# Gated linear attention into a routed expert layer: a table in its own tile, another order of loads, and ScalarE's and VectorE's order in the first steps

## The chip, the cores and the metric

The kernel runs on one core of one Trainium2 chip. Such a core has five engines that each work through their own queue in order: TensorE (PE, matrix products), VectorE (DVE), ScalarE (ACT, functions such as exp and ln), GpSimd (POOL) and SyncE (SP, which here only issues loads and stores). They wait for each other through semaphores; an instruction that waits holds up all that stands behind it on its engine. 16 DMA engines move data between the device memory (HBM) and the on-chip memory (SBUF). TensorE writes into PSUM, a small memory[...]. The metric is the device time of one launch in microseconds (us).

## The reference

Two blocks follow one another. The first is attention with a decaying state: for each of 4 batches and 8 heads, 768 tokens of width 48,

```python
f = 1.0 / (1.0 + np.exp(-f_logit))
for t in range(S):
    state = f[:, :, t, :, None] * state + np.einsum('bhd,bhe->bhde', k[:, :, t], v[:, :, t])
    y[:, :, t] = np.einsum('bhd,bhde->bhe', q[:, :, t], state)
```

Its output, 3072 rows of 384, goes into a layer of 8 experts. Each row takes the expert with the largest logit of `x @ w_gate`, with the softmax weight of that expert, and yields `gate_w * (relu(x @ w1[e]) @ w2[e])`, w1 being 384 x 1024 and w2 1024 x 384. All is in float32.

## The kernel before

**Units.** The attention is cut into 12 units: a unit is one chunk of 128 tokens of two batches, all 8 heads. Its q, k and f are tiles of 128 partitions x 8 segments x 128 tokens (512 KB each), its v is 384 KB. Within a chunk the recurrence becomes matrix products. For unit u:

- `steps` (L486, its exp at L492 and its ln, `log`, at L500): ScalarE makes ln(1 + exp(-f)), the decay of each token; `part` is a half of the segments, and `ab` names both halves.
- `total` (L502, instruction at L507): VectorE's running sum of it, a scan.
- `growth` (L516): ScalarE's exp of the sum, the tile r. `by_r` (L523): k times r, in place. It runs on GpSimd but for unit 0. `decay` (L533): exp of minus the sum. `by_decay` (L545): q times that, on VectorE.
- `ends` (L530) and `last_decay` (L540): small copies on GpSimd.
- `score` (L553): 32 matrix products of q and k. `mask` (L563): VectorE copies the causal half out of PSUM, in four instructions. `within` (L581): scores times v, the part of the output from the own chunk, in two halves.
- `keys` (L567), `keep` (L577): k is transposed on TensorE, and copied to SBUF by ScalarE.
- `added` (L617, PE dp): the state that the chunk adds; `update` (L633): VectorE adds it to the old state, GpSimd multiplies by the last decay. `before` (L596): q times the old state.
- `settle` (L645): ScalarE copies the output out of PSUM. `rows` (L660): TensorE turns it into rows and makes the gate's logits with the same products (PE xp, L679); VectorE sums the logits (lg, L687). `lay` (L697): ScalarE copies the rows.
- `Route.choose`, `place`, `fill` (L222 to L271): small VectorE instructions that pick the expert and the place of each row, for two units at a time. `send` scatters the rows by GpSimd.

**Steps.** The loop of L817 is a software pipeline: step n works on `score` to `added` of unit n, on the preparation of units n+1 to n+3, and on the output of units n-1 and n-2. The order of the source lines is the order of each engine's queue (`manual_schedule`, L711); nothing is reordered afterwards. Ahead of the loop stand the preparation of units 0 to 2 and `warm` (L721), matrix products whose result is not used.

**Buffers that set the order.** f has 2 tiles, k and v 3, q 4; r and the copied output one. The PSUM tiles of `keys`, `rows` and `added` take turns in two slots (`turns`, L468), so `added` of a step waits until `lay` has copied the first rows tile of that step. SP issues the loads in the order of the `load` calls (L473); a load into a tile that is still being read waits, and holds up those behind it.

**Constants.** `fpack` holds the float constants side by side: the unit matrix `ident` first, and among the others the table "rows" of 4 x 112 columns, which has a unit matrix for each half of the partitions with room for the gate's weights around it. `load_gate` (L176) writes these weights into the table, and so waits for the load of the table. `mpack` is the causal mask.

**`routed`.** L526 to L528 tie a k times r to an earlier VectorE instruction: it does not start before that has ended.

**After the attention** each expert's rows are read back, transposed and put through the two products by TensorE (L333, L349), with rows beyond the fixed regions in quarters of tiles (L1099, L1125). The change does not touch this.

## Time and profile before

| | |
|---|---|
| runs shown: median (lowest to highest of 3) | 394.76 us (393.43 to 395.92) |
| profiled execution: its time | 389.92 us |
| profiled execution: span from first to last instruction | 387.9 us |
| mean granted TensorE clock | 0.999 |
| TensorE busy | 375.7 us (97%) |
| VectorE busy | 169.3 us (44%) |
| ScalarE busy | 103.1 us (27%) |
| GpSimd busy | 116.0 us (30%) |
| moved by DMA | 95.04 MB |

The profile is of one execution. Its rows name an engine, a line of the kernel, an operation and the tiles it writes and reads, with the number of instructions and the time of one. In the timeline a row has its start and duration, and in brackets how long the engine had been idle and what ended that. SPq and POOLq are the DMA-issuing sides of these engines. A busy share is an average over the attention, which is over at about 125 us, and the experts; the stretch of the change is the first 45 us.

### The profile page before, as it was taken

What the parts mean: (1) busy time and instruction counts of PE and PEld (TensorE: products, weight loads), DVE (VectorE), ACT (ScalarE), POOL (GpSimd) and SP (SyncE); (2) the same over time, 40 slices, a digit from 0 to 9 for tenths busy, and PEclk for the clock granted to TensorE, in tenths of its full rate; (3) what the DMA queues carried; (4) which work ended last, traced back from release to release, by engine and by line L of the source; (5) the groups of instructions that cost most, each with busy time, mean ns of one, the idle gap of its engine ahead of it and who ended that gap; (6) DMA issues with size and microseconds to landing.
All of it is one profiled execution on the core that took longest, in us unless ns stands there. A gap on an engine that the chain in (4) does not pass through costs nothing.

```text
span 387.9 us, 7721 instructions
## 1 busy us (share of the span) xinstructions
PE 375.7 (97%) x3062; PEld 264.0 (68%) x3062; DVE 169.3 (44%) x365; ACT 103.1 (27%) x190; POOL 116.0 (30%) x118
## 2 busy tenths in 40 slices
PE   7899999999999999999999999999999999999994
PEld 7778899999989778685555555654466456555452
DVE  6899988889764632112121131115412113111260
ACT  6998878785433001010100110000010000001000
POOL 5378868887745410101102101100210210210112
PEclk9999999999999999999999999999999999999999
DMA  7999667778983459695659899899164449994151
GB/s 284 383 376 349 219 221 251 249 239 297 391 310 114 169 149 325 157 318 108 196 156 382 221 393 395 209 403 250 41 222 136 102 178 390 396 417 159 20 186 43
DMA packets 51515, 95.04 MB, mean 245 GB/s; under 512 B 20824, under 2 KB 40731, under 8 KB 49424
## 3 DMA queue, kind: packets, MB, share of 16 engines
q1 hardware_dynamic: 48016, 84.76, 64.4%
q0 software_dynamic: 3168, 9.64, 6.6%
q8 instruction: 25, 0.41, 0.5%
q14 instruction: 18, 0.15, 0.1%
q10 hardware_dynamic: 288, 0.08, 0.1%
HBM read 79.46 MB, written 15.21 MB: 244 GB/s over the span
## 4 chain that ended last, share of the span: by engine, by line
PE 88%; DMA 5%; DVE 2%; SPq 1%; issue 1%; ACT 1%; POOL 0%; POOLq 0%; DVEq 0%; ACTq 0%
PE hps L333 28%; PE yps L349 24%; PE yps L1125 7%; PE xp L679 6%; PE yt L587 5%; PE s L559 4%; PE s L333 3%; PE hps L1099 3%; PE yp L349 3%; PE yt L608 3%; DMA fpack<-c_fpack 2%; DMA f<-in_fu_dram 2%; PE dp L624 2%; PE kp L574 2%; DMA fpack<-in_moe_w_gate_dram 1%; SPq L482 1%
## 5 line engine op out<-in xcount | busy, mean ns | idle before, releaser
L333 PE MATMUL hps<-xT,w1t 128*128 128x352 f32 (+2 forms) x384 | 110.1, 447 | 0.0
L333 PEld LDWEIGHTS hps<-xT,w1t 128*128 128x128 f32 x384 | 72.7, 190 | 37.2 <-issue 1.9
L349 PE MATMUL yps<-w2t,hT 128*128 128x384 f32 x288 | 94.4, 487 | 0.0
L192 POOL DMA_INDIRECT out_dram<-ysb,dst x24 | 23.3, 972 | 224.4 <-DVE ysb L360 216.2
L349 PEld LDWEIGHTS yps<-w2t,hT 128*128 128x128 f32 x288 | 54.6, 190 | 38.6 <-issue 1.5
L343 ACT ACTIVATE hT<-hps 128x352 f32<-128x352 f32 (+2 forms) x28 | 13.7, 490 | 200.7 <-PE hps L333 190.6
L345 DVE TENSOR_SCALAR hT<-hps 128x352 f32<-128x352 f32 (+2 forms) x28 | 15.6, 558 | 93.0 <-PE hps L333 93.0
L360 DVE TENSOR_SCALAR ysb<-yps,tg 128x384 f32<-128x384 f32 x22 | 13.6, 618 | 74.4 <-PE yps L349 55.7
L192 POOL DMA_INDIRECT xs<-xr,posi x24 | 32.3, 1346 | 16.5 <-issue 4.8
L565 DVE COPY_PREDICATED at<-mpack,s 128x512 f32<-128x512 uint8 x48 | 31.1, 730 | 6.1 <-PE s L559 6.1
L525 POOL TENSOR_TENSOR k<-k,r 128x1024 f32<-128x1024 f32 (+1 forms) x12 | 26.6, 2217 | 19.2 <-ACT r L521 9.8
L507 DVE TENSOR_TENSOR_SCAN sum<-g,cap 128x1032 f32<-128x1032 f32 (+1 forms) x14 | 28.9, 2061 | 3.3 <-ACT g L500 3.2
L559 PE MATMUL s<-q,k 64*128 64x128 f32 x384 | 24.9, 279 | 2.4 <-POOL last L543 1.6
L1125 PE MATMUL yps<-qw,hqT 128*32 128x192 f32 (+1 forms) x192 | 26.8, 380 | 0.0
L679 PE MATMUL xp<-fpack,ys 128*128 128x104 f32 x192 | 25.1, 281 | 0.5 <-DMA fpack<-in_moe_w_gate_dram 0.3
L559 PEld LDWEIGHTS s<-q,k 64*128 64x128 f32 x384 | 22.5, 188 | 4.6 <-POOL last L543 1.8
L587 PE MATMUL yt<-at,v 128*48 128x128 f32 x384 | 25.1, 276 | 0.0
L679 PEld LDWEIGHTS xp<-fpack,ys 128*128 128x128 f32 x192 | 22.7, 191 | 2.4 <-issue 1.9
L587 PEld LDWEIGHTS yt<-at,v 128*48 128x48 f32 x384 | 20.0, 123 | 2.6 <-issue 1.3
L1125 PE MATMUL yps<-w2t,hT 128*32 128x384 f32 x192 | 21.4, 487 | 0.0
L1125 PEld LDWEIGHTS yps<-w2t,hT 128*32 128x32 f32 x192 | 7.6, 110 | 13.0 <-issue 12.5
L548 DVE TENSOR_TENSOR q<-q,g 128x1024 f32<-128x1024 f32 (+1 forms) x14 | 16.1, 1159 | 0.1
(114 smaller groups left out, 359.8 us busy)
## 6 DMA issues: line engine op xcount, KB each, us to landing
qw<-in_moe_w_dram SPq DMA_DIRECT2D x16, 1536.0 KB, 8.9
w1t<-in_moe_w_dram SPq DMA_DIRECT2D x8, 1536.0 KB, 7.5
w2t<-in_moe_w_dram SPq DMA_DIRECT2D x8, 1536.0 KB, 6.9
k<-in_ku_dram SPq DMA_DIRECT2D x12, 512.0 KB, 4.6
q<-in_qu_dram SPq DMA_DIRECT2D x12, 512.0 KB, 8.4
f<-in_fu_dram SPq DMA_DIRECT2D x11, 512.0 KB, 7.3
xs<-pad SPq DMA_DIRECT2D x8, 600.0 KB, 4.5
v<-in_vu_dram SPq DMA_DIRECT2D x12, 384.0 KB, 5.9
```

The costliest lines, as they stand in the source:

```text
L192: ins = nc.gpsimd.indirect_dma_start(out=dst, out_offset=bass.IndirectOffsetOnAxis(ap=idx, axis=0), in_=src, in_offset=None, bounds_check= ...
L333: nc.tensor.matmul(x["h"][:, f], lhsT=w[0][:, j, b * 128 : b * 128 + 128], rhs=x["xT"][:, j], start=j == 0, stop=j == KD - 1,)
L345: nc.vector.tensor_scalar(to, x["h"], 0.0, None, op0=OP.max)
L349: nc.tensor.matmul(yp, lhsT=x["hT"][:, f, t * C : t * C + C], rhs=w[1][:, f, :], start=f == 0, stop=f == NF - 1,)
L507: nc.vector.tensor_tensor_scan(x["sum"][:, part].rearrange("p s c -> p (s c)"), x["g"][:, part].rearrange("p s c -> p (s c)"), cap[:, part ...
L525: ins = on.tensor_tensor(k, k, units[u]["r"][:, part], op=OP.mult).ins
L548: nc.vector.tensor_tensor(q, q, x["dec"][:, part], op=OP.mult)
L559: done["score"] = nc.tensor.matmul(ps[h][:, p], lhsT=x["k"][r, s], rhs=x["q"][r, s], start=True, stop=True).ins
L565: nc.vector.copy_predicated(x["at"][:, a, h], _bc(causal, 1, HP), x["ps", a][h])
L587: nc.tensor.matmul(x["yt"][DP * (h ^ a) : DP * (h ^ a) + D, a, p], lhsT=x["v"][:, a, 2 * p + h], rhs=x["at"][:, a, h, p], start=p == 0, st ...
L679: done["rows"] = nc.tensor.matmul(xp[:, p], lhsT=x["ys"][:, a, p], rhs=wx[:, p, 0:XW] if a else wx[:, p, E:WX], start=True, stop=True,).ins
L1125: nc.tensor.matmul(yp[r], lhsT=h[:, f, at : at + T], rhs=w[:, f, cols], start=f == 0, stop=f == NF - 1, skip_group_check=True,)
```

## The change

The table "rows" leaves `fpack` and becomes a tile of its own, `wx`: GpSimd clears it at the start, and `lay_selection` copies the two unit matrices into it from `ident` once unit 0 is prepared. The gate's loads go into this tile. `ident` and `mpack` are loaded from SP's queue instead of ScalarE's. The order of loads becomes f0, k0, first half of f1, q0, second half of f1, ident, mpack, k1, q1 and so on; the gate is loaded ahead of f4, k3, q3, v2 and f5, the other constants after them.

In the preparation, q times decay of unit 0 comes after both halves of k times r. The masks of unit 0 are put between the halves of unit 1's preparation, whose second k times r waits for the first half's q times decay. `warm` has 8 products instead of 12.

In steps 1 to 3: k times r of unit 3 goes to VectorE, ahead of the last of step 2's four masks. exp and ln of units 4, 5 and 6 are issued apart: the ln of units 4 and 5 comes a step after the exp, that of unit 6 at the end of step 3, and in steps 2 and 3 they stand behind `lay`. `growth` of units 4 and 5 moves: that of unit 4 from step 2 into step 3, that of unit 5 to the end of step 3. `total(5)` and `choose` go behind `update(3)`, `settle(2)` from the start of step 4 to the end of step 3. Later steps are as before.

```diff
@@ -97,11 +97,6 @@
         "p": p[:, None],
         "sel": np.stack([p < DP, p >= DP], 1),
     }
-
-    sel = np.zeros((128, HP, WX))
-    for a in range(2):
-        sel[DP * a + np.arange(D), :, E + D * a + np.arange(D)] = 1.0
-    f["rows"] = sel.reshape(128, HP * WX)
 
     for n in (1, 2, 4):
         f[f"run{n}"] = row(np.tile(np.arange(n + 1) > 0, E))
@@ -161,13 +156,20 @@
     rend = cpool.tile([128, NU, SEG], F32, name="rend")
     gsum = cpool.tile([128, NU, 2], F32, name="gsum")
     pad = cpool.tile([128, ROW], F32, name="pad")
-    wx = const("rows").rearrange("p (h w) -> p h w", w=WX)
+    wx = cpool.tile([128, HP, WX], F32, name="wx")
     halves = [(a, slice(DP * a, DP * a + D)) for a in range(2)]
     fdram = nc.inline_tensor(fv, name="c_fpack").ap()
 
     def load_first_consts():
-        nc.scalar.dma_start(mpack, nc.inline_tensor(mv, name="c_mpack").ap())
-        nc.scalar.dma_start(ident, fdram[:, slice(*fat["ident"])])
+        nc.sync.dma_start(ident, fdram[:, slice(*fat["ident"])])
+        nc.sync.dma_start(mpack, nc.inline_tensor(mv, name="c_mpack").ap())
+
+    def lay_selection():
+
+        for a, r in halves:
+            nc.gpsimd.tensor_copy(
+                wx[r, :, E + D * a : E + D * a + D], _bc(ident[r, DP * a : DP * a + D], 1, HP)
+            )
 
     def load_consts():
         at = fat["ident"][1]
@@ -184,6 +186,7 @@
 
     nc.gpsimd.memset(pad, 0.0)
     nc.gpsimd.memset(pad[:, TOK : TOK + 1], float(FAR))
+    nc.gpsimd.memset(wx, 0.0)
 
     early_reads = []
     SYNC = mybir.DependencyInfo(mybir.DependencyClass.Sync, mybir.DependencyReason.DATA)
@@ -523,7 +526,7 @@
         def by_r(u, part=whole, on=nc.gpsimd):
             k = units[u]["k"][:, part]
             ins = on.tensor_tensor(k, k, units[u]["r"][:, part], op=OP.mult).ins
-            if routed:
+            if routed and on is nc.gpsimd:
 
                 tc.add_manual_dep(ins, routed.pop().name, SYNC, reason="the port of both")
 
@@ -545,7 +548,7 @@
         def by_decay(u, part=whole):
             x = units[u]
             q = x["q"][:, part]
-            nc.vector.tensor_tensor(q, q, x["dec"][:, part], op=OP.mult)
+            return nc.vector.tensor_tensor(q, q, x["dec"][:, part], op=OP.mult).ins
 
         def heads():
             return [(p, h, slice(DP * h, DP * h + DP)) for p in range(HP) for h in range(2)]
@@ -712,8 +715,10 @@
 
         nc.scalar.preload_act_table_set("natural_log_exp_and_others")
         load(0, "f", ab)
-        load(0, "kq")
-        load(1, "f")
+        load(0, "k")
+        load(1, "f", ab[:1])
+        load(0, "q")
+        load(1, "f", ab[1:])
         load_first_consts()
         load(1, "kq")
         for i in (1, 0):
@@ -733,16 +738,18 @@
             growth(0, part)
             by_r(0, part, nc.vector)
             decay(0, part)
+        for part in ab:
             by_decay(0, part)
         ends(0)
         last_decay(0)
+        lay_selection()
         for part in ab:
             steps(1, part)
         load(3, "f")
         load(2, "k")
         load(1, "v")
         load(2, "q")
-        load(3, "q")
+        load_gate()
 
         def early_banks():
 
@@ -788,31 +795,31 @@
         score(0, 0)
         score(0, 1)
         keys(0)
-        warm(12)
+        warm(8)
         for part in ab:
             total(1, part)
-        for a in range(2):
+        for a, part in enumerate(ab):
+            growth(1, part)
+            by_r(1, part)
+            decay(1, part)
             for h in range(2):
                 mask(0, a, h)
-        for part in ab:
-            growth(1, part)
-            by_r(1, part)
-        for part in ab:
-            decay(1, part)
-            by_decay(1, part)
+            scaled = by_decay(1, part)
+            if a == 0:
+                routed.append(scaled)
         ends(1)
         last_decay(1)
         steps(2)
+        load(4, "f")
+        load(3, "k")
+        load(3, "q")
+        load(2, "v")
         total(2)
         keep(0)
         steps(3, logs=False)
         growth(2)
+        load(5, "f")
         load_consts()
-        load(3, "k")
-        load(4, "f")
-        load(2, "v")
-        load(5, "f")
-        load_gate()
 
         for n in range(1, NU + 2):
             here, back, last = n, n - 1, n - 2
@@ -821,14 +828,14 @@
             rt = None
             if here < NU:
                 units[here]["old"] = states[here % 2]
-            if 2 <= last:
+            if 2 < last:
                 settle(last)
             if later and later[0] < NU - 1:
                 later[1].weigh()
             if here < NU:
                 for a in range(2):
                     score(here, a)
-            if ahead and n != 2:
+            if ahead and not 1 < n < 4:
                 by_r(n + 1)
                 ends(n + 1)
             if decayed:
@@ -850,28 +857,32 @@
             if state:
                 keys(here)
                 keep(here)
-            if n == 2:
+            if 1 < n < 4:
                 growth(n + 1)
-                by_r(n + 1)
+                if n == 3:
+                    by_r(n + 1)
                 ends(n + 1)
-            if 1 < n < 4:
                 decay(n + 1)
                 last_decay(n + 1)
             if here < NU:
                 for a in range(2):
                     for h in range(2):
+                        if n == 2 and a and h:
+                            by_r(n + 1, on=nc.vector)
                         mask(here, a, h)
             if n == 1:
                 log(3)
                 within(0, 0)
                 within(0, 1)
                 settle(0)
-            if n + 3 < NU:
+            if n == 1:
+                steps(4, logs=False)
+            elif n > 3 and n + 3 < NU:
                 steps(n + 3)
             if later and n >= NU - 1:
                 settled(*later)
                 later = None
-            if 2 < n < NU - 2:
+            if 3 < n < NU - 2:
                 total(n + 2)
             if n == NU - 2:
                 by_decay(n + 1)
@@ -881,6 +892,9 @@
             if 0 <= last:
                 rt = rows(last, later[1] if later else None)
                 lay(last)
+            if 1 < n < 4:
+                log(n + 2)
+                steps(n + 3, logs=False)
             if n == NU + 1:
                 scatter_some("rows")
             if later and n == NU - 2:
@@ -890,9 +904,9 @@
                 by_decay(n + 1)
             if n == 2:
                 total(n + 2)
-            if rt:
+            if rt and n != 3:
                 rt.choose()
-                if n < NU - 2:
+                if 3 < n < NU - 2:
                     routed.append(rt.latest)
                 if n >= NU - 1:
                     rt.weigh()
@@ -905,7 +919,7 @@
                     within(back, a)
             if n == 2:
                 settle(1)
-            if n + 2 < NU and n != 1:
+            if n + 2 < NU and n > 3:
                 growth(n + 2)
             if n == NU + 1:
                 widen(soon[0], weights[0], early_h, range(3, 7))
@@ -916,8 +930,16 @@
                 decayed = update(here)
             if n == 1:
                 total(3)
+            if n == 3:
+                total(5)
+                rt.choose()
+                routed.append(rt.latest)
             if back < NU:
                 before(back)
+            if n == 3:
+                settle(2)
+                log(6)
+                growth(5)
             if NU - 1 <= n <= NU:
                 scatter_some("before")
             if rt:
```

## The prediction

> **What bounds the kernel now.** I read the page first, for where TensorE (PE) stops being the only bound.
>
> ```profile
> span 387.9 us, 7721 instructions
> ...
> PE   7899999999999999999999999999999999999994
> ...
> DVE  6899988889764632112121131115412113111260
> ```
>
> Each digit is a tenth of one fortieth of the span, 9.7 us. PE is full from the third slice on; VectorE (DVE) is full in slices two to five, and near empty once the experts run. So the change, which touches the first 45 us, can only bring PE's full stretch forward. The chain that ended last, in order of time (start, duration, what), says who delays PE before that:
>
> ```profile
> 29.25 2.02 PE xp L679 x16
> 31.27 0.02 issue
> 31.29 0.04 DVE lg L687
> 31.33 0.07 issue
> 31.40 1.68 DVE q L548
> 33.08 1.16 DVE sum L507
> ...
> 38.26 1.97 DVE sum L507
> 40.22 0.78 issue
> 41.00 0.17 DVE lg L687
> 41.17 0.02 issue
> 41.19 0.49 ACT xr L709
> 41.68 0.04 issue
> 41.72 1.14 PE dp L624 x32
> ```
>
> From 41.72 the chain is PE work to the end, but for single microseconds. What is to be costed is therefore when `added(3)` (dp, L624) starts, and whether PE stays fed after it. Last the timeline (start, duration, engine, line; in brackets the idle time before):
>
> ```profile
> 9.81 0.64 ACT L492 ACTIVATE g<-f 128x512 f32<-128x512 f32 x1 [0.68 <-DMA f<-in_fu_dram]
> 11.22 2.51 DVE L507 TENSOR_TENSOR_SCAN sum<-g,cap 128x516 f32<-128x516 f32 x2 [0.73 <-ACT g L500]
> ...
> 36.53 2.38 POOL L525 TENSOR_TENSOR k<-k,r 128x1024 f32<-128x1024 f32 x1 [1.04 <-ACT r L521]
> 38.15 2.93 DVE L507 TENSOR_TENSOR_SCAN sum<-g,cap 128x1032 f32<-128x1032 f32 x1
> 47.50 2.29 DVE L507 TENSOR_TENSOR_SCAN sum<-g,cap 128x1032 f32<-128x1032 f32 x1
> ```
>
> VectorE works from 11.22 to 44.5 with only 1.4 us of gaps: it is the bound of this stretch. Its scan `total` (L507) takes 2.29 alone, and 2.93 where it starts while GpSimd's k times r (36.53 to 38.91) still has 0.76 to go; q times decay (L548) likewise 1.22 alone (at 50.46) and 1.68 at 31.40.
>
> **The change, part by part.** I walk VectorE's queue and shift it.
>
> *Loads.* The windows move 0.97 MB by 5.0 us and 2.88 MB by 10.0. f of unit 1 lands at 9.78; it and all ahead of it are 2.18 MB, reached at about 8.3, so a load lands some 1.5 us after its bytes' turn. In the new order f1's first half ends at 1.31 MB (turn 6.1, lands 7.6), q0 at 1.84 MB (8.9), f1's second half at 2.10 MB (9.6). ScalarE is busy until 9.12 with unit 0, so `steps(1)` starts at 9.12 instead of 9.81, and the first logarithm ends at 10.5 instead of 11.19. [...] The trace has the case: f0's first half was usable 3.2 us after its issue (exp at 4.02), while the whole f1 took 7.17. What counts is the first half's turn, so I take the trace: 0.7 us.
>
> q0's 0.18 MB more ahead of it costs 0.5; it was used at 8.59, so it lands by 9.05 at worst. q times decay of unit 0 now stands behind both k times r, at 9.3: covered by 0.3 us, beyond which each microsecond late is one on VectorE. ident and mpack move from ScalarE's queue into SP's at 2.1 MB and land near 9.8 instead of 4.9; first users are the `keys(0)` transposes at 11.7 and mask(0) at 13.0. Their two issues (0.43 each) hold k1 and q1 up in a queue that has 2 MB outstanding: nothing. The 448 columns less of the table are 0.23 MB, 0.6 us of transfer; nobody on the path waits for those bytes any more, so between 0 and 0.6, taken as 0. The gate's four loads (SP waited 2.7 us for the table ahead of them and issued until 24.5; landed 29.16) now wait only for a memset done by 5.5, and land near 20.5, ahead of `rows(0)`. They stand ahead of f4, k3, q3 and v2; beside the gate's packets throughput fell for 1 us from 344 to 229 GB/s, so I charge 0.6 us: f4 at 22.1, wanted at 24.1; k3 at 23.6, wanted at 28.6. The constants behind f5 land near 27.5, wanted by `choose` at 43 and by GpSimd's token copy, at 35.2 before. Nothing.
>
> *GpSimd.* memset of wx: 448 columns by pad's row (400 columns, 0.43) is 0.5, in an idle stretch from 4.7 to 8.0. Two copies of `lay_selection` are in no row: nearest is L531's small copy, 0.19 free and up to 2.2 when it is held up beside a scan. I take 0.3 each. GpSimd idled 3.27 us ahead of its k times r at 13.20; the cover is 1.5 us beyond ident's landing.
>
> *Steps 0 and 1.* total(1) then runs 10.5 to 13.0. mask(0) and q times decay by halves take 3.73 as before, to 16.75 (was 17.38). k times r of the second half now waits for the first q times decay (14.9) and ends at 16.4; behind it on GpSimd are only small copies until 20, and score(1) needs q at 16.7 anyway. warm(8) takes 8/12 of 2.84, so 1.9, ending at 14.7, before score(1) can start at 15.0. total(2) 16.8 to 19.1, mask(1) to 22.3, q times decay to 23.75, total(3) to 26.75, each about 0.95 earlier: 0.7 from f1 and 0.25 of gaps (17.38 to 17.66) closed.
>
> *Step 2.* k times r of unit 3 on VectorE: not in the trace. Below, twice the half at 0.62; above, L548 held up, 1.75. It is the same form as L548, so 1.22. It needs r, for which ScalarE goes through score(2) from 23.9, half of keys(2), keep(2) 1.05 and growth(3) 1.05, to 28.55; VectorE comes to it at 28.65 after three masks (0.65 each). So no wait, but a cover of only 0.1: a late r holds the fourth mask, both reductions and all behind. k times r to 29.9, fourth mask 30.5, first lg 30.7, lay's first copy 31.2. ScalarE's exp and log (2.2 us) no longer stand ahead of lay, and the gate no longer holds `rows(0)`: dp(2) starts at 31.2 (was 33.03). Then q times decay(3) to 32.1, not held up by GpSimd's k times r. log(4) now comes behind lay, 31.4 to 32.5, so total(4) waits 0.4 and runs 32.5 to 34.8 (was 33.00 to 35.30).
>
> *Step 3.* mask(3) to 37.8, lg to 38.65, with total(5) no longer ahead. PE took 8.69 from dp(2) to dp(3), 0.56 of it a stall for lay, which goes: dp(3) at 31.2 + 8.13 = 39.35 (was 41.72), **2.4 us** gained. But update(3), total(5), choose now stand in VectorE's queue behind dp(3), which ends at 40.5: 0.55 + 2.30 + 1.17, to 44.5, then mask(4) at 44.5 (was 45.01). What is late next is there: mask(4) 2.6, total(6) 2.3, lg 0.2, lay 0.5 set dp(4) at 50.05. PE alone would be there at 49.0. So 1.0 us is given back; dp(4) was at 51.15 to 51.3 and keeps some **1.3 us**. In step 5 PE's wide rows end after total(7), and dp(5) is not held: VectorE waits 0.6 us per step for scores in the later steps (row at 72.69), so it catches up.
>
> **The sum.** The profiled execution took 389.92, 387.9 of it the span: minus 1.3 to 1.4 gives 388.6. The runs shown have their median 4.84 above it, at 394.76; I carry the same difference over: **393.4**.
>
> **The rivals.**
> *No give-back.* If score and mask of step 4 overlap better, or total(5) starts before dp(3) has ended, the 2.4 us of dp(3) stay: 392.4. VectorE's own work caps this: 33.8 us from 11.22 to mask(4), less 1.9 idle, plus 1.22 for k times r, less 1.1 of hold-ups removed, is 32.0; from 10.5 that is 42.5, 2.5 earlier, and with lay's 0.85 of slack at dp(4) at most 3.3 us: 391.4. For it: the gaps I left in the queue sum to 1.9. Against: the order as written puts total(5) behind update(3).
>
> *VectorE pays (slower).* It is the bound, gets 1.22 more, and waits 0.4 for log(4) and up to 0.5 for dp(3). The walk has it 0.5 early at mask(4) only because 0.7 of f1 and 1.1 of hold-ups come off. If they don't (f1's half lands with the rest, GpSimd's copies still lie beside scans), mask(4) starts at 45.01 + 1.3 = 46.3 and dp(4) 5.6 later, at 51.9: 0.6 later than before, 395.4. It decides from mask(4) at 45.7 on (51.3 less 5.6); a late r adds one for one past 0.1. For it: VectorE's full digits, and a cover of 0.1. Against: f0's halves, and the 1.22 of L548 wherever GpSimd is quiet.
>
> *Nothing arrives at the end*, since a later stage waits for something else: 394.8. Against: PE has no gap from 42 to the experts, and the weights' loads follow PE's own releases.
>
> **How the numbers follow.** Forecast 393.4, 50%; no give-back 392.0 in the middle, 22%; VectorE pays 15%; nothing 13%. All of them lie within 1% of 394.76, which is about what a measurement of this kernel can tell from no change. More than 1% (3.9 us) needs more than the cap of 3.3, or the timed runs, which are slower than the profiled one, to gain more from early loads than the trace shows: 9%. Slower by 1% needs a head of a queue that is held for 5 us: 4%. Range 391.3 to 395.5: from the cap to most of the slower case.
>
> **What would show it.** Right: exp of unit 1 without idle at 9.1; scan of unit 1 at 10.5; no wait of xp for the gate; dp(2) near 31.2, dp(3) near 39.4, then a PE wait of about 1 us for lay at dp(4), near 50. Wrong: k times r of unit 3 waiting for r on VectorE, q0 holding VectorE at 9.3, PE waiting for lay at dp(5) too, or f4 landing after 24.

## The result, and the profile after

The changed kernel takes 392.83 us in the median of 22 runs (391.8 to 396.09), the kernel before 394.79 in 22 runs beside it (392.57 to 395.92): ratio 0.9965 [0.9949, 0.998], 1.96 us less. The forecast was 393.4, in a range of 391.3 to 395.5. The number was met. Much of its sum was not, and the experiments below are about that.

The page of the changed kernel; its profiled execution took 393.27 us:

```profile
span 391.5 us, 7712 instructions
...
DVE  6998998979663632112121131116413013111450
```

VectorE is still full in slices two to five, only in other slices of them. The span is 3.6 us longer than that of the profile before, in a kernel whose runs are faster. This is the first sign that the two profiles can't be subtracted: they come from chips of two kinds. On one kind the kernel before takes 389.7 us, on the other about 394 (the experiments below). By these times the profile before was taken on the first kind, the timed runs and the profile after on the second.

The chain that ended last, for the changed kernel (start, duration, what):

```profile
2.62 6.55 DMA q<-in_qu_dram
...
27.69 0.96 ACT r L524
...
31.03 0.55 ACT xr L707 x2
31.58 0.96 ACT g L503
...
32.63 0.06 DVE sum L510
...
41.60 2.30 DVE sum L510
...
44.98 2.51 DVE at L568 x4
47.49 1.78 DVE sum L510
49.27 0.40 issue
49.67 0.26 DVE lg L690 x2
```

Before, the chain became PE work at 41.72. Now VectorE's scans and masks carry it past 49.67, and it leaves them only in the next step. The new order brought step 2 forward, and VectorE then could not follow. The same in the timeline of the changed kernel (start, duration, engine, line; in brackets the idle time before):

```profile
8.64 0.61 ACT L495 ACTIVATE g<-f 128x512 f32<-128x512 f32 x1
9.19 1.29 DVE L551 TENSOR_TENSOR q<-q,g 128x512 f32<-128x512 f32 x2 [0.25 <-DMA q<-in_qu_dram]
10.40 2.60 DVE L510 TENSOR_TENSOR_SCAN sum<-g,cap 128x516 f32<-128x516 f32 x2
28.67 1.23 DVE L528 TENSOR_TENSOR k<-k,r 128x1024 f32<-128x1024 f32 x1
31.19 1.14 PE L627 MATMUL dp<-v,kn 128*64 128x48 f32 x32 [0.25 <-ACT xr L712]
32.63 2.31 DVE L510 TENSOR_TENSOR_SCAN sum<-g,cap 128x1032 f32<-128x1032 f32 x1 [0.78 <-ACT g L503]
35.45 0.66 PE L577 MATMUL kp<-fpack,k 128*128 128x128 f32 x4 [0.55 <-DVE state L644]
39.92 1.09 PE L627 MATMUL dp<-v,kn 128*64 128x48 f32 x32
46.72 1.14 PE L682 MATMUL xp<-wx,ys 128*128 128x104 f32 x8 [0.67 <-ACT kn L582]
50.40 1.14 PE L627 MATMUL dp<-v,kn 128*64 128x48 f32 x32 [0.19 <-ACT xr L712]
56.17 2.78 DVE L510 TENSOR_TENSOR_SCAN sum<-g,cap 128x1032 f32<-128x1032 f32 x1
59.60 1.14 PE L627 MATMUL dp<-v,kn 128*64 128x48 f32 x32
```

The `added` products of units 2 to 5 (L627; L624 before; dp(2) to dp(5) from here on) start at 31.19, 39.92, 50.40 and 59.60; before at 33.03, 41.72, 51.15 and 60.08. So 1.84 us is gained at the first, 1.80 at the second, 0.75 at the third, 0.48 at the fourth. PE's new waits are those for the PSUM slot that dp(2) had filled (35.45), for kn, the copy of k that ScalarE makes for unit 4 (46.72), and for lay (50.40). The second is no wait for VectorE: ScalarE works without a gap from 42.15 on, and has `settle(2)`, the logarithm of unit 6 and `growth(5)`, all put there by the change, ahead of this copy.

### The profile page after: what moved, and what is told of

Its sections match the earlier page's. It is cut to its first block, busy times and chain, and to the rows that moved or that the text cites. A ratio compares the mean times of both kernels' runs of the same rounds, so it can differ in the third digit from the quotient of the medians.

```text
span 391.5 us, 7712 instructions
## 1 busy us (share of the span) xinstructions
PE 377.9 (97%) x3054; PEld 264.7 (68%) x3054; DVE 171.0 (44%) x366; ACT 102.8 (26%) x190; POOL 113.7 (29%) x120
## 4 chain that ended last, share of the span: by engine, by line
PE 84%; DVE 8%; issue 2%; DMA 2%; ACT 1%; POOL 1%; SPq 0%; POOLq 0%; DVEq 0%; ACTq 0%
PE hps L336 28%; PE yps L352 24%; PE yps L1147 7%; PE xp L682 5%; PE yt L590 4%; PE s L562 4%; PE s L336 3%; DVE sum L510 3%; PE hps L1121 3%; PE yt L611 2%; PE yp L352 2%; DVE at L568 2%; DMA q<-in_qu_dram 2%; DVE q L551 1%; PE kp L577 1%
## 5 line engine op out<-in xcount | busy, mean ns | idle before, releaser
L528 POOL TENSOR_TENSOR k<-k,r 128x1024 f32<-128x1024 f32 (+1 forms) x11 | 24.1, 2190 | 14.1 <-ACT r L524 7.1
L682 PE MATMUL xp<-wx,ys 128*128 128x104 f32 x192 | 25.2, 281 | 0.9 <-ACT kn L582 0.7
L682 PEld LDWEIGHTS xp<-wx,ys 128*128 128x128 f32 x192 | 22.7, 191 | 2.8 <-issue 1.4
```

The source lines that it names most:

```text
L528: ins = on.tensor_tensor(k, k, units[u]["r"][:, part], op=OP.mult).ins
L682: done["rows"] = nc.tensor.matmul(xp[:, p], lhsT=x["ys"][:, a, p], rhs=wx[:, p, 0:XW] if a else wx[:, p, E:WX], start=True, stop=True,).ins
```

## The experiments

The theory after the result: the early gain is given back in steps 3 to 5, most of all on VectorE, and the timed difference has another source than that gain. The rivals: the timed difference is the gain at dp(4) and dp(5), plus something in the later kernel; or the difference belongs to the chip. The runs fell on chips of both kinds, so each is compared with the kernel before on its own chip, and starts only within one kind.

**Both kernels again (before2, after2, before3).** No edit: the kernel before twice more, the changed one once more.

> The kernel before, unchanged, looked at a second time, to see what repeats from one execution to the next. Theory (the prediction's): dp(2), dp(3) and dp(4) start at 33.0, 41.7 and 51.2 again, within 0.2, since every wait there comes from an order and from durations. Rival (a stall of TensorE that comes and goes in the later part decides the total): the starts up to 62 us repeat, but the time between the early expert tile and the end moves by 1 to 4 us.

> The changed kernel, unchanged, looked at a second time. Theory: dp(2), dp(3), dp(4), dp(5) at 31.2, 39.9, 50.4, 59.6 again, within 0.2. The wait of 1.3 us between the early tile's first and second product (near 127 us) and the lost 0.3 us in steps 5, 7 and 9 were in one profile: if they belong to the change they are there again, if they belong to the execution they are gone or elsewhere, and the span falls by some 2 to 3 us.

> The kernel before, unchanged, a third time, for the clock. The timed runs of before on the chip of the record fall into two groups, 392.6 to 394.0 with a granted clock of 0.995 or more and 394.2 to 395.7 mostly at 0.991 to 0.992. Theory [...]: where this execution is of the slow group, windows of 1 us show 0.50 in steps 2 to 3, score(3) takes 3.6 instead of 2.0, and dp(4) comes 1.7 us later than 51.1; where it is of the fast group, dp(2) to dp(4) are as before. Rival (the two groups come from the tail of the kernel): the clock is 1.00 up to 380 us in either case.

The first two ran on one chip of the first kind: before 389.72 (ratio to itself 1.0003 [0.9994, 1.0012]), changed 389.96 against 389.67, ratio 1.0006 [0.9997, 1.0015]. On this chip the change brings nothing. On a second chip of that kind before took 389.81 against 389.74, 0.9998 [0.999, 1.0005]. Timeline of the kernel before in its second profile:

```profile
33.00 1.14 PE L624 MATMUL dp<-v,kn 128*64 128x48 f32 x32 [1.13 <-ACT xr L709]
...
51.11 1.09 PE L624 MATMUL dp<-v,kn 128*64 128x48 f32 x32
...
60.04 1.09 PE L624 MATMUL dp<-v,kn 128*64 128x48 f32 x32
```

And of the changed kernel on the same chip:

```profile
31.48 1.14 PE L627 MATMUL dp<-v,kn 128*64 128x48 f32 x32 [0.24 <-ACT xr L712]
...
50.67 1.14 PE L627 MATMUL dp<-v,kn 128*64 128x48 f32 x32 [0.18 <-ACT xr L712]
...
56.48 2.75 DVE L510 TENSOR_TENSOR_SCAN sum<-g,cap 128x1032 f32<-128x1032 f32 x1
59.88 1.14 PE L627 MATMUL dp<-v,kn 128*64 128x48 f32 x32
```

The gain is 1.52 us at dp(2), 0.44 at dp(4), 0.16 at dp(5). These are pairs of single executions, which differ by as much: on the second chip of that kind the kernel before starts dp(2) at 33.57 and dp(5) at 60.60, some 0.56 later than above. In the changed kernel part of this spread has one source. q of unit 0 now stands behind half of f1, and VectorE waits for it, by 0.25 in the profile after, by 0.64 here, and by 0 to 0.86 in the edited kernels below; all that follows moves with it. At the first expert it is 0.11 (142.64 against 142.75), and at the end of PE still 0.11 (381.96 against 382.07). Yet the span is 0.7 longer. From the start of the last scatter on, 382.82 before and 382.72 after, the rest of the span takes 4.78 and 5.58. The queue of the instruction loads from 385 us on (number, MB, share of the DMA engines), before:

```profile
q14 instruction: 2, 0.02, 0.6%
```

and after:

```profile
q14 instruction: 3, 0.02, 0.7%
```

One more load of instructions falls into the end (five instead of four from the last scatter on). So 0.1 us of the span is gained on PE, and 0.8 lost behind it. Not all of this is in the time: between span and time lie 2.0 us in the runs of before and 1.8 in those of the changed kernel. The waits near 127 us and in steps 5, 7 and 9 that the profile after has are gone here, so they don't belong to the change.

**Three more GpSimd instructions, nothing else (pool3).** In the kernel before, three repeats of a small memset:

```diff
     nc.gpsimd.memset(pad, 0.0)
+    for _ in range(3):
+        nc.gpsimd.memset(pad[:, USED:ROW], 0.0)
```

> The kernel before with three small memsets more on GpSimd at its start, where it idles (columns of pad that are zero already). In all profiles so far the stretch from the last scatter's start to the end of the span is 4.8 to 5.0 us with four 8 KB instruction loads in it (before), and 5.4 to 5.8 with five (every kernel with the table's own tile, which has three GpSimd instructions more). Theory [...]: with three GpSimd instructions more the tail is 5.4 to 5.8 with five loads, and the time 0.4 to 0.6 above before. Rival (something else of the new tile makes the tail longer): 4.8 to 5.0, four loads, and the time of before.

Measured 393.25 against 393.67 on a chip of the second kind, 0.998 [0.9965, 0.9994]. The part of the span behind the last scatter (386.36 to 391.9) takes 5.54 with five instruction loads, as in the changed kernel, and not 4.8 to 5.1 with four. So three more GpSimd instructions are enough for a longer end. That the fifth load is what lengthens it is not shown: two edited kernels below, those with both edits at once and with the later scans moved, have four loads behind the last scatter and need 5.82 and 5.78 all the same. Nor do the runs show the price. A time 0.4 to 0.6 longer was expected, and the median fell by 0.4; part of before's runs on this chip are slow for another reason, taken up below, and the others have their median at 393.19, 0.06 below these.

**The halves of f of unit 1 undone (load_old).** On the changed kernel:

```diff
-        load(0, "k")
-        load(1, "f", ab[:1])
-        load(0, "q")
-        load(1, "f", ab[1:])
+        load(0, "kq")
+        load(1, "f")
```

> The changed kernel with the first loads in the old order (f0, k0, q0, f1 as one transfer). Theory (f1's first half is worth 0.7 us on VectorE): the exp of unit 1 starts at 9.7 to 9.8 instead of 8.6 to 9.1, its scan at 11.2, dp(2) near 31.9 and dp(4) near 51.0; the time 0.6 to 0.7 longer than the changed kernel's. Rival (it is absorbed by a gap further on): dp(2) stays at 31.2.

Measured 390.61 against 389.67 for the kernel before, 1.0023 [1.0015, 1.0031]. Timeline of this kernel:

```profile
32.26 1.14 PE L627 MATMUL dp<-v,kn 128*64 128x48 f32 x32 [0.24 <-ACT xr L712]
```

All dp start 0.78 to 0.79 us later than in the changed kernel on this chip, and the time is 0.65 longer. The split in two halves is worth its 0.7 us, and this gain comes through to the end undiminished. It would be larger if q of unit 0 came in time, for which VectorE does not wait here.

**k times r of unit 3 back on GpSimd (kr3_pool).** On the changed kernel:

```diff
-                if n == 3:
-                    by_r(n + 1)
+                by_r(n + 1)
                 ends(n + 1)
...
-                        if n == 2 and a and h:
-                            by_r(n + 1, on=nc.vector)
                         mask(here, a, h)
```

> The changed kernel with k times r of unit 3 back on GpSimd. Theory (the move trades 1.22 us of VectorE for two hold-ups and lands near nought): VectorE is free 1.2 us earlier for the fourth mask, q times decay of unit 3 is held up by GpSimd to 31.1 + 1.2, score(3) starts at 32.2 to 32.4 as with the move, total(4) 0 to 0.3 earlier; dp(4) at 50.1 to 50.4. Rival (the move is what brings the gain): dp(3) and dp(4) come 1 us later or more.

Measured 389.16 against 389.67, 0.9986 [0.9978, 0.9995]: 0.8 us faster than the changed kernel on the same chip, where the theory had nothing. Timeline of this kernel:

```profile
49.73 1.14 PE L627 MATMUL dp<-v,kn 128*64 128x48 f32 x32 [0.19 <-ACT xr L712]
...
58.93 1.14 PE L627 MATMUL dp<-v,kn 128*64 128x48 f32 x32
```

dp(4) is 0.94 us earlier than in the changed kernel, dp(5) 0.95. Of this 0.40 is there at dp(0) already (17.95 for 18.35), ahead of the edit, since VectorE waited only 0.18 for q of unit 0. That leaves 0.54. So the 1.23 us on VectorE cost 0.5 to 0.8 us. GpSimd's 2.4 us for the same product stand beside other work but for 0.45, for which PE waits at the scores of unit 3.

**The logarithm of unit 4 back ahead of lay (log4_early).** On the changed kernel:

```diff
             if n == 1:
-                steps(4, logs=False)
+                steps(4)
...
             if 1 < n < 4:
-                log(n + 2)
+                if n == 3:
+                    log(n + 2)
```

> The changed kernel with the ln of unit 4 right behind its exp in step 1, not behind lay in step 2. Theory (VectorE's gap ahead of total(4) is real loss on the bound): total(4) starts at 31.9 instead of 32.6, dp(3) near 39.3, dp(4) near 49.7, 0.7 earlier. Rival (ScalarE in step 1 is what it costs, keep(2) and growth(3) come later): k times r of unit 3 waits for r up to 0.6, and dp(4) is not earlier.

Measured 393.91 on a chip of the second kind, 0.9984 [0.9963, 1.0004]: unclear. Timeline of this kernel:

```profile
39.67 1.09 PE L627 MATMUL dp<-v,kn 128*64 128x48 f32 x32
...
50.23 1.14 PE L627 MATMUL dp<-v,kn 128*64 128x48 f32 x32 [0.19 <-ACT xr L712]
```

The first scores start at 10.52, and at 9.94 in the profile of the changed kernel, 0.58 later, as q of unit 0 came late by that much more. Taken from there, dp(2) (31.70) stands where it stood, dp(3) and dp(4) are 0.8 earlier. So the wait of `total(4)` for its logarithm, 0.78 in the timeline after, does cost what it says at dp(4); in the time it is not shown.

**Both at once (kr3_log4).** The last two edits together.

> The changed kernel with k times r of unit 3 back on GpSimd and the ln of unit 4 right behind its exp. Theory (both edits of the change put VectorE later, and each alone gave back 0.7 to 0.9 us at dp(4)): dp(2) near 30.7, dp(3) near 38.8, dp(4) 49.0 to 49.7, the time 1.0 to 1.6 us below the changed kernel's on the same chip. Rival (they give back the same gap once): dp(4) no earlier than 49.7, the time 0.8 below.

Measured 389.03 against 389.74, 0.9981 [0.9972, 0.9991], the lowest median of all. Timeline of this kernel:

```profile
50.12 1.14 PE L627 MATMUL dp<-v,kn 128*64 128x48 f32 x32 [0.20 <-ACT xr L712]
```

With both undone the kernel is 0.7 us below before, with k times r alone 0.5, on another chip, and the two intervals overlap. dp(0) starts at 18.36 here, as in the changed kernel's profile of this kind (18.35), and dp(4) 0.55 earlier than there: no more than the 0.54 of k times r alone. So the rival holds: the two edits of the change take away the same gap in VectorE's queue, once.

**The scan of unit 5 ahead of step 3's rows (tot5_old).** On the changed kernel, as the kernel before had it:

```diff
+            if n == 3:
+                log(5)
-            if 3 < n < NU - 2:
+            if 2 < n < NU - 2:
                 total(n + 2)
...
             if 1 < n < 4:
-                log(n + 2)
+                if n == 2:
+                    log(n + 2)
...
             if n == 3:
-                total(5)
                 rt.choose()
```

> The changed kernel with the ln and the scan of unit 5 back ahead of the logit sums of step 3. Theory (dp(3)'s gain is partly given back at dp(4) because the scan now stands behind update(3)): lg of step 3 waits for the scan, dp(3) starts near 40.9 instead of 39.9, but mask(4) starts near 43.8 instead of 44.9 and dp(4) near 50.0 instead of 50.4: the move of the scan is worth nothing or costs 0.4. Rival (the 2.4 us of dp(3) are the gain): dp(4) comes 0.5 to 1 us later than in the changed kernel.

Measured 398.18 against 394.04, 1.0102 [1.0065, 1.0138]: slower by more than any theory had it. Timeline of this kernel:

```profile
38.80 1.04 ACT L503 ACTIVATE g<-g 128x1024 f32<-128x1024 f32 x1
39.95 2.62 DVE L510 TENSOR_TENSOR_SCAN sum<-g,cap 128x1032 f32<-128x1032 f32 x1 [1.77 <-ACT g L503]
42.49 0.26 DVE L690 TENSOR_REDUCE lg<-xp 128x8 f32<-128x32 f32 x2
43.21 1.72 PE L627 MATMUL dp<-v,kn 128*64 128x48 f32 x32 [2.85 <-ACT xr L712]
46.75 3.75 PE L562 MATMUL s<-q,k 64*128 64x128 f32 x32
```

The logarithm comes only at 38.80, behind what ScalarE has to do in that step, so the scan waits 1.77 us at the head of VectorE's queue, with lg and lay behind it, and PE waits 2.85. Then something more happens: dp takes 1.72 instead of 1.14, the scores 3.75 instead of 2.06. The same kernel by stretches of time (length; busy time and instructions of PE, its weight loads, VectorE, ScalarE and GpSimd; the granted TensorE clock; DMA share; GB/s):

```profile
42.00:43.00 1.00, 0.00 (x0) 0.00 (x0) 1.00 (x4) 0.32 (x1) 0.68 (x2) 1.00 0.72 286
43.00:44.00 1.00, 0.79 (x20) 0.79 (x21) 0.88 (x1) 1.00 (x4) 0.00 (x0) 0.76 0.02 6
44.00:46.00 2.00, 2.00 (x42) 1.91 (x44) 0.96 (x4) 0.65 (x2) 0.00 (x0) 0.50 0.04 8
46.00:48.00 2.00, 2.00 (x28) 1.64 (x22) 0.56 (x4) 1.06 (x3) 0.00 (x0) 0.50 0.13 20
48.00:50.00 2.00, 2.00 (x22) 2.00 (x22) 1.14 (x2) 2.00 (x5) 0.00 (x1) 0.50 0.94 338
50.00:51.00 1.00, 1.00 (x11) 0.81 (x10) 0.67 (x2) 0.98 (x2) 1.00 (x1) 0.83 0.82 332
```

The clock was 0.50 from about 43.5 on, for some 6.8 us (estimated from the 0.76 and 0.83 at its ends). At half the clock this is a loss of about 3.4, by estimate. Two of the seven executions, with a mean clock of 0.998 and 0.999, took 396.5, so that without the fall this edit still costs some 3 us against the 393.5 of before's executions with a clock of 0.994 or more.

**The later scans behind lay (tot_late).** On the changed kernel:

```diff
-            if 3 < n < NU - 2:
-                total(n + 2)
             if n == NU - 2:
...
-            if n == 2:
+            if n == 2 or 3 < n < NU - 2:
                 total(n + 2)
```

> The changed kernel with the scan of steps 4 to 9 behind q times decay, as it is in step 2, instead of ahead of the logit sums. Theory (the scan of unit 6 ahead of the logit sums is what holds dp(4)): lg of step 4 at 48 to 49, dp(4) near 49.4 without a wait for lay, 1.0 earlier; in later steps VectorE, which has 0.3 to 0.6 us a step to spare, keeps up, and the whole is 0.5 to 1.0 us shorter than the changed kernel. Rival (VectorE's sum of work is the bound, so the wait only moves on): mask(5) and with it dp(5) come 1 us late instead, and the time is that of the changed kernel.

Measured 395.87, 1.0057 [1.0038, 1.0076]. Timeline of this kernel:

```profile
49.87 1.09 PE L627 MATMUL dp<-v,kn 128*64 128x48 f32 x32
...
59.20 1.13 PE L627 MATMUL dp<-v,kn 128*64 128x48 f32 x32
```

dp(4) and dp(5) start 0.53 and 0.40 earlier than in the profile after (0.17 of that is there at dp(2) already), and PE does not wait at dp(4). It still waits 0.67 for kn ahead of it, as in the changed kernel: with VectorE out of the way only 0.36 of the 1.05 comes back at dp(4), and what ScalarE's order costs there no run isolates. From dp(5) on the four intervals are 9.82, 9.35, 9.88 and 9.83 us, in the profile after 9.69, 8.93, 9.69 and 8.93. So the wait has only moved on, as the rival had it; it grows there, and the time is longer, not the same.

**The gate and the table's own tile, without the rest (gate_only).** On the kernel before (with the table taken out of the constants as in the change, not shown again):

```diff
+    nc.gpsimd.memset(wx, 0.0)
...
         last_decay(0)
+        lay_selection()
...
+        load_gate()
         load_consts()
         load(3, "k")
         load(4, "f")
         load(2, "v")
         load(5, "f")
-        load_gate()
```

> The kernel before with only the table's own tile: table out of the constants, gate's weights loaded ahead of the constants, all else in the old order. Theory: rows(0) no longer waits 0.3 us for the gate, but dp(2) is set by lay behind ScalarE's exp and ln, so dp(2) stays at 32.9 to 33.0, dp(4) at 51.1 to 51.3, and the time is the same within 0.2. Rival (the gate's late landing and SP held for 2.7 us are what the change removes): dp(2) and dp(4) 0.5 us earlier or more.

Measured 395.87 against 394.04, 1.004 [1.0018, 1.0063]: alone this part is slower, where both theories had no loss. Timeline of this kernel:

```profile
27.15 1.06 ACT L495 ACTIVATE g<-f 128x1024 f32<-128x1024 f32 x1 [2.45 <-DMA f<-in_fu_dram]
29.92 2.03 PE L682 MATMUL xp<-wx,ys 128*128 128x104 f32 x16 [1.27 <-ACT kn L582]
34.80 1.14 PE L627 MATMUL dp<-v,kn 128*64 128x48 f32 x32 [1.84 <-ACT xr L712]
35.87 3.69 PE L562 MATMUL s<-q,k 64*128 64x128 f32 x32
```

f of unit 4 stands behind the gate's loads and the constants here, and ScalarE waits 2.45 us for it. Its exponential starts at 27.15; in the kernel before at 25.38, in the changed kernel at 23.88 without a wait, since f4 is ahead of the constants there. PE then waits 1.27 and 1.84 us. The same kernel by stretches:

```profile
33.00:34.00 1.00, 0.00 (x0) 0.00 (x0) 1.00 (x1) 0.97 (x3) 1.00 (x2) 1.00 1.07 402
34.00:35.00 1.00, 0.20 (x6) 0.20 (x8) 1.00 (x2) 1.00 (x4) 1.00 (x2) 1.00 0.89 337
35.00:36.00 1.00, 1.00 (x34) 0.94 (x30) 1.00 (x1) 1.00 (x3) 1.00 (x1) 0.96 0.93 347
36.00:37.00 1.00, 1.00 (x10) 1.00 (x12) 1.00 (x2) 0.16 (x1) 1.00 (x2) 0.50 1.07 328
...
38.00:39.00 1.00, 1.00 (x12) 1.00 (x12) 1.00 (x2) 0.19 (x1) 0.73 (x1) 0.50 0.70 263
39.00:40.00 1.00, 1.00 (x12) 0.87 (x10) 0.73 (x2) 0.00 (x0) 1.00 (x1) 0.84 0.28 115
```

Again 0.50, from about 35.9 on for some 3.4 us (estimated from the 0.96 and 0.84 at its ends), and scores of 3.69 instead of 2.06. The six executions with a mean clock of 0.994 or more have their median at 394.9, those of before at 393.5: the late f4 costs without the fall too.

**A wait made longer in the kernel before (act_extra).** Three copies of 0.47 us on ScalarE ahead of lay in step 2:

```diff
+            if n == 2:
+                for _ in range(3):
+                    nc.scalar.copy(scr, cap.rearrange("p s c -> p (s c)")[:, 0:320])
             if 0 <= last:
                 rt = rows(last, later[1] if later else None)
```

> The kernel before with three idle ScalarE copies of 320 columns (some 1.1 us together) put ahead of lay in step 2, so that TensorE waits some 1.9 us for lay at dp(2) instead of 0.8. Theory [...]: in some or all executions the mean clock is 0.991 to 0.992, the profile shows 0.50 in steps 2 to 3 with score(3) at 3.6 us, and the time is 1.1 us above before without, and near 2.8 us above it with the fall[...]. Rival (the fall needs more than this, or another chip): clock as before, time 1.0 to 1.2 us above before in all executions.

Measured 395.03 against 393.67, 1.0026 [1.0001, 1.0051]. Timeline of this kernel:

```profile
32.55 1.42 ACT L884 COPY scr<-cap 128x320 f32<-128x320 f32 x3
...
34.41 1.14 PE L625 MATMUL dp<-v,kn 128*64 128x48 f32 x32 [2.06 <-ACT xr L710]
```

In this profile the clock did not fall. But of its 12 executions 8 have a mean clock of 0.989 to 0.993 and take 394.76 to 395.93; the other 4 have 0.995 to 0.997 and take 392.85 to 393.84. Of the kernel before on the same chip 10 of 31 lie below 0.994. So low means came more often with the longer wait, 8 of 12 against 10 of 31, and not in every execution; with so few executions this is at the edge of chance. The expected 1.1 us without the fall did not come: the median of the 4 is 393.31, that of before's 21 executions at 0.994 or more 393.19.

**What the profiles show of the clock.** In two of them it fell to 0.50 within the steps. In gate_only PE had waited 1.27 and 1.84 us ahead of it, in tot5_old 2.85. In the kernel with the three copies PE waited 2.06 us, and the clock stayed at 1.00:

```profile
32.00:34.00 2.00, 0.35 (x8) 0.09 (x2) 2.00 (x2) 1.94 (x5) 2.00 (x3) 1.00 1.04 383
34.00:36.00 2.00, 1.59 (x40) 1.54 (x42) 1.66 (x2) 2.00 (x6) 1.52 (x3) 1.00 0.94 306
36.00:38.00 2.00, 2.00 (x33) 1.88 (x30) 1.55 (x4) 0.72 (x1) 1.20 (x1) 1.00 1.02 404
```

So a wait of PE stood ahead of both falls, and one longer than gate_only's had no fall behind it. What lets the clock fall, and why some executions of a kernel have a low mean and others not, is not shown.

**What this says of the timed difference.** The runs of the record, sorted:

| | executions | up to 394 us | their median | above 394 us | their median |
|---|---|---|---|---|---|
| before | 22 | 9 | 393.09 | 13 | 395.23 |
| changed | 22 | 20 | 392.78 | 2 | 395.19 |

Between the lower groups there are 0.3 us. The other 1.65 of the 1.96 is that the median of before lies in its upper group, and that of the changed kernel in its lower one. Of before's runs here the clocks are not known, but on two chips of the second kind they are. On chip 3, 10 of its 31 executions have a mean clock below 0.994 (median 395.0) and 21 a higher one (393.19); on chip 7, 13 of 39 (394.70, the others 393.49). By estimate, one stretch like that of gate_only, 3.4 us at half the clock, costs 1.7 us, close to the 1.8 between the groups on chip 3, and lowers the mean clock by 0.5 x 3.4 / 388 = 0.0044, somewhat less than the 0.0055 between the groups' means. The mean is a rough sign: it takes in a fall behind the last product too (in after2 0.59 from 384 to 386 us and 0.50 from there on), where PE has nothing left to do, and after2 has a mean of 0.995. Of the changed kernel's 22 executions none lies below 0.994, and the two above 394 us have 0.994 and 0.998. On the two chips of the first kind no execution of either kernel lies below 0.994 (of load_old's 20 there one does, with 0.991 and 392.12 us), and there the change shows nothing.

Whether the new order removed falls of the clock is not shown. For it: it shortens PE's waits for lay in step 2 from 0.76 to 1.24 us (four profiles of before's order) to 0.25, and in step 3 from 0.55 to none. Against it: the kernel with three memsets, whose waits in these steps are those of before, has no mean below 0.994 among 20 executions; and log4_early, whose waits are as short as the changed kernel's, has 4 among 12. No profile caught the kernel before in a fall, so whether and where it has one is open. Nor is step 2 the only place where PE waits. All seven profiles of the second kind have PE waiting between 126 and 135 us, where the first expert products begin, by 0.8 to 1.75 us in all, and none of the first kind does. The row of the kernel with three memsets:

```profile
129.17 5.43 PE L351 MATMUL yp<-w2t,hT 128*128 128x384 f32 x16 [1.24 <-ACT hT L345]
```

Whether the clock falls there in any execution was not shown.

## Why the prediction was right or wrong

**The number was right by luck, and not by its sum.** The sum took 1.3 to 1.4 us off the profiled execution and carried the 4.84 us between it and the timed runs over as a constant. That is the step that failed. Some 3.4 of the 4.84 lie between the two kinds of chips (389.7 and the lower group's 393.09); most of the rest is that before's median lies in the upper group. On the first kind, that of the profile, the sum makes 388.6, and the changed kernel takes 389.96 there, 0.3 above before with an interval that takes in no difference. On the second kind 0.3 of the 1.3 us arrived between the lower groups. The rest of the 1.96 is that fewer runs lie in the upper group, for which the prediction had no term; that the clock is behind it is likely, and not shown for these runs.

**Loads: f1 right, q0 mis-sized.** The prediction had exp(1) at 9.1 and scan(1) at 10.5; they start at 8.64 and 10.40 (exp(0) too was earlier in that execution, 3.62 instead of 4.02). The split of f1, taken from f0's halves in the trace, was worth 0.65 to 0.8 us. For q of unit 0 it had a cover of 0.3 at 9.3. There was none: VectorE was ready at 8.94 and waited 0.25 in the profile after and 0.64 in after2, which is one of the signs of being wrong that it named. This load is on the chain that ended last.

**The gate at 0.6 us, too small.** In gate_only it stands ahead of f4, which ScalarE waits for in both kernels, and f4 comes 1.77 us later (27.15 for 25.38). The forecast came off unharmed: in the changed kernel f4 is ahead of the constants, and exp(4) starts at 23.88 without a wait.

**Step 2, right to the hundredth by luck in part.** dp(2) 31.19 for 31.2. k times r started at 28.67 for 28.65 and took 1.23 for 1.22. The cover of 0.1 was gone: the third mask ended at 28.60 and r at 28.64, so VectorE waited for r, if only for hundredths. On the chip of the profile before dp(2) starts at 31.48.

**k times r on VectorE, mis-sized.** It was walked through as one term among others and not priced alone. Alone it costs 0.54 us at dp(4) and 0.8 in the runs, and the kernel is faster without it.

**log(4) behind lay, 0.4 expected, 0.78 measured.** The logarithm ended at 32.53, as forecast (32.5); VectorE was free for it at 31.86 instead of 32.1. log4_early shows that the wait is paid in full at dp(3), as long as k times r stands on VectorE too.

**Step 3, 0.57 late.** dp(3) 39.92 for 39.35: the prediction's "8.13 of PE from dp(2) to dp(3)" had no wait in it, and there is one of 0.55. The second half of `keys(3)` waits for VectorE's update to read dp(2) and free its PSUM slot, and that update stands behind the late `total(4)`. The wait of lay did go, as predicted.

**The give-back, right in size, half right in kind.** The prediction had mask(4) at 44.5 and dp(4) at 50.05; they start at 44.90 and 50.40. PE's 10.48 from dp(3) to dp(4) is 1.05 more than before's 9.43, as the 1.0 of the forecast. But its kind is only half right: the forecast was one wait of about 1 us for lay, and PE waits 0.19 for lay and 0.67 for kn, which stands behind ScalarE's new order. ScalarE's queue at the end of step 3 had no term in the walk.

**"dp(5) is not held", wrong.** total(7) runs beside GpSimd's product and takes 2.78 (56.17), dp(5) is held by about 0.3 and keeps 0.48, on the other chip 0.16, and 0.11 at the experts. The prediction argued from VectorE's idle time in later steps, but dp(5) comes before these.

**The end, not thought of.** 5.4 to 5.8 us of span behind the last scatter instead of 4.8 to 5.1, less the 0.2 that is not in the time. That is some 0.45 (an estimate from these spans), more than PE keeps on the first kind of chip; pool3's runs show less, 0.06.

**Rivals.** "VectorE pays" named the mechanism that took the gain, with a price of 0.6 over before; on one chip of the first kind the changed kernel is 0.3 above before, in an interval that takes in no difference. "Nothing arrives at the end" is what that chip shows. "No give-back" falls.

## What to carry to other kernels

A stall removed ahead of the engine that is the bound is worth only what that engine can follow (1.84 us at dp(2) here, 0.48 of it left at dp(5)): walk its queue on until the gain is either kept for several steps or gone, and price each operation that is moved to it by itself. Ask of each load that is put ahead of another who waits for the other. Before the distance between a profile and timed runs is carried over, look whether both are of one chip and whether the runs have one group or two. Two versions within half a per cent are told apart only on the same chip (the kernel before took 389.7 us on the one kind and 393.7 to 394.8 on the other).

## What the runs showed of the hardware

- **TensorE's granted clock fell to half in the steps of two profiles.** In gate_only it was 0.50 from about 35.9 us on for some 3.4 us, after PE had waited 1.84 us for lay; in tot5_old from about 43.5 on for some 6.8 us, after a wait of 2.85. The scores took 3.69 and 3.75 us there instead of 2.06. In act_extra PE waited 2.06 us and the clock stayed at 1.00. What lets it fall is open.
- **Chips differ by 4 us in one kernel.** 389.7 on two chips, 393.7 to 394.8 on the others. The changed kernel's two profiles, one of each kind, differ by 0.28 us at dp(5) (59.60 and 59.88, the other way round) and by 3 us at the last scatter (385.67 and 382.72). Some of it goes in each second step (from dp(5) to dp(6) 9.69 us on the one, 9.43 on the other), some near 127 us, where PE waits 0.52 and the releaser shown is "issue". The cause is open.
- **The end of a kernel can depend on three small instructions.** With three more on GpSimd the span behind the last scatter took 5.4 to 5.8 us in ten profiles, and 4.8 to 5.1 in four without them; in pool3 nothing else was changed. In eight of the ten a fifth instruction load of 8 KB falls into this stretch, in two it does not; what lengthens it is open.
- **Two copies of 48x192 on GpSimd** took 1.67 us together (10.25 in the profile after) beside a VectorE scan (0.6 had been estimated). They ended at 11.92, ahead of the r that GpSimd's next product waits for (12.44).
